# Softmax sums of a recurrent attention chain, issued in column groups of 32, with fewer filler matmuls

## The chip, the core and the metric

The kernel runs on one core of a Trainium2 chip. The metric is device time in microseconds (us), as the median of the runs. TensorE's instructions are written PE (matmuls) and PEld (weight loads), VectorE is DVE, ScalarE is ACT, GpSimd is POOL, and SP is the engine that issues most of the DMA transfers.

## The reference, cut to what matters

The model is four layers, A, B, A, B, on x of 2048 rows by 640 columns. Layer A is attention in 64 segments of 32 rows, each with 8 memory rows ahead of it. The memory rows of a segment are the first 8 output rows of the segment before, so the segments are a chain.

```python
for s in range(n_seg):                       # 64 segments, 32 heads of 192
    h = concatenate([mem, x[:, 32*s:32*s+32]], axis=1)      # 40 rows of 640
    q, k, v = h @ Wq, h @ Wk, h @ Wv
    p = softmax(where(mask, q @ k.T * scale, -1e9))
    o = (p @ v) @ Wo
    mem = o[:, :8]
    outs.append(o[:, 8:])
x = x + concatenate(outs)      # layer A; layer B follows (linear attention), then both again
```

## The kernel before, in words

Each layer A first computes, for all segments at once, the parts of q, k and v that do not depend on the memory (`A_pre`). Then `A_chain` walks through the 64 segments. A segment goes through four rounds of 8 heads each, in the order 0 to 3 or, in every second segment, 3 to 0.

**Order.** `A_chain` runs under a manual schedule: each engine works through its instructions in the order in which the code issues them, and semaphores hold them where they depend on another engine or a DMA transfer. So the order below is the code's order.

**A segment.** The new rows lie transposed in `hT` (128 partitions, five blocks of 32 columns). `project` multiplies them by a round's weights for Q, K or V: five steps of four matmuls each, one matmul for each group of 32 output partitions (`tile_position=(0, 32 * g)`, line 988), each 32 columns of weights from `hT` and 384 moving columns. ACT copies the result out of `ps_qk` into `raw` (line 998; one buffer, used for Q and K in turn), and DVE transposes `raw` into `QT` (lines 1006 to 1008) or `KT` (1003). For V, ACT and DVE (1017, 1019) copy to `Vp`, whose rows 64 to 79 a DMA fills from `vb` (`extra_v`, line 971, issued by POOL).

`scores` (mask matmul line 1025, six matmuls line 1030) fills `ps_s`, ACT takes the exponential into `E` (line 1085), and `sums` (line 1099) multiplies `E` (80 partitions, 320 columns) by a block of ones, which leaves each column's sum in the 80 partitions of `ps_s`. `normalise` takes ln and exp of the negative of these sums on ACT (1104, 1105), and DVE multiplies `E` by the result (1106). `attend` (line 1038) multiplies `E` by `Vp`; ACT and DVE (1044, 1045) copy to `OT`; `wo_round` (line 1067) multiplies `OT` by a round's output weights and adds up in `ps_w`: twelve steps of four matmuls with 160 columns, again one for each group of 32 output partitions. The mask, the scores, the sums, `attend` and the fillers use the whole array; `project` and `wo_round` use column groups of 32.

Round n of a segment runs Q of n+1, `attend` of n-1, scores of n, K of n+1, sums of n, V of n+1. The last round has no following projections: behind V of round 3 stand scores, `attend` of round 2, part of a `wo_round`, sums, the rest of the `wo_round`s, four filler matmuls (`keep_busy`, line 1074, into `ps_idle`, which nothing reads), `attend` of round 3, five fillers, the last `wo_round`, five fillers and two weight loads (`fill`, line 1080). Then DVE transposes `ps_w` (line 1220) and casts it into the first eight columns of the next `hT` (1221), and the next segment begins. Between these, DVE also transposes the next segment's own rows into `hT` (line 943).

**Loads.** Part of the weights stays in SBUF. In each segment SP loads again three blocks each of Wq, Wk and Wv (line 681) as the projections of round 0 give their slots free, and the output weights of the last round (line 698, six transfers of 320 KB), into the buffer `wo_end`, which the `wo_round` of the first round has just read. POOL issues the small transfers of `vb`, `kqb` and `otb`.

**Fillers.** A segment holds a fixed number of TensorE instructions. The first segment of the first layer A also has `FILL[0]` weight loads of a single column.

Of the kernel before, what the change touches and what calls it, by code (L numbers as in the profile page):

```python
# [17 lines left out]
SLOTS = {"Q": 3, "K": 3, "V": 3}  # L18
LN_EPS = 1e-5

FILL = {0: 86, 2: 79}
SEG_FILL = 2

LATE = 64512
# [3 lines left out]
def ap3(ap, dims):  # L28
    return bass.AP(tensor=ap.tensor, offset=ap.offset, ap=[list(d) for d in dims])
# [86 lines left out]
class Kernel:  # L116
# [799 lines left out]
    def A_chain(self, xn_dram, at_dram, li, load_slot, piece, load_wo, late_wo, wo_mid, wo_end, low):  # L916
        nc, tc, KC, NSEG = self.nc, self.tc, self.KC, self.NSEG
        scale = float(self.Dh) ** -0.5
        NR = 4
        with tc.tile_pool(name=f"A{li}_ch", reuse_waits="tile", bufs=1) as sp, \  # L920
# [17 lines left out]
            def load_rows(s):  # L938
                nc.gpsimd.dma_start(out=xr[8:32, :], in_=xn_dram[32 * s:32 * s + 24, :])
# [61 lines left out]
            def to_rows(raw, m):  # L1001
                if m == "K":
                    nc.vector.transpose(out=KT[:, :, 0:64], in_=raw[:, :].rearrange("p (c j) -> p c j", j=64))  # L1003
                else:
                    rv = raw[:, :].rearrange("p (x i j) -> p x i j", i=3, j=64)
                    nc.vector.transpose(out=QT[:, :, 0:4:3, 0:64], in_=rv[:, :, 0:3:2, :])  # L1006
                    nc.vector.transpose(out=QT[0:64, :, 1, 0:64], in_=rv[0:64, :, 1, :])
                    nc.vector.transpose(out=QT[64:P, :, 2, 0:64], in_=rv[64:P, :, 1, :])
# [25 lines left out]
            def attend(E, n, OT=None):  # L1034
                O = [pop.tile([P, 512], F32, name=f"ps_o{x}", tag=f"o{x}") for x in range(2)]
                for x in range(2):
                    for k, e, i in ((0, 0, 0), (320, 1, 2), (128, 0, 1), (192, 1, 1)):
                        nc.tensor.matmul(O[x][:, 80 * i:80 * i + 80], lhsT=Vs[n % 2][0:80, 448 * x + k:448 * x + k + 128],  # L1038
                                         rhs=E[0:80, 160 * x + 80 * e:160 * x + 80 * e + 80], start=(k == 0),
                                         stop=(k == 192), skip_group_check=True)  # L1040
                if OT is None:
                    OT = sp.tile([P, 6, 64], BF16, name="OT", tag="OT")
                o = [x[:, 0:240].rearrange("p (i q) -> p i q", q=80) for x in O]
                nc.scalar.activation(out=OT[:, 0:3, :], in_=o[0][:, :, 0:64], func=ACT.Copy)  # L1044
                nc.vector.tensor_copy(out=OT[:, 3:6, :], in_=o[1][:, :, 0:64])
                return OT, o
# [15 lines left out]
            def wo_round(W, r, OT, first, last, part=range(12)):  # L1062
                w = low[:, 0:7680] if last_wo == r else wo_end[:, :] if r in (0, 3) else wo_mid[:, 7680 * (r - 1):7680 * r]
                for i in part:
                    c, q = i % 6, 32 * (i // 6)
                    for g in range(4):
                        nc.tensor.matmul(W[32 * g:32 * g + 32, 0:160], lhsT=OT[:, c, q:q + 32],  # L1067
                                         rhs=w[:, 640 * i + 160 * g:640 * i + 160 * g + 160], start=(first and i == 0),
                                         stop=(last and i == 11), tile_position=(0, 32 * g), skip_group_check=True)

            def keep_busy(ps, n, w=384):

                for _ in range(n):
                    nc.tensor.matmul(ps[:, 0:w], lhsT=self.ident[:, :], rhs=wo_mid[:, 0:w], start=True, stop=True,  # L1074
                                     skip_group_check=True)

            def fill(n):

                for _ in range(n):
                    nc.tensor.ldweights(self.ident[:, 0:1])  # L1080

            def weigh(last):
                S = scores()
                E = sp.tile([P, 384], BF16, name="E3", tag="raw") if last else sp.tile([P, 320], BF16, name="E", tag="E")
                nc.scalar.activation(out=E[0:80, 0:320], in_=S[0:80, 0:320], func=ACT.Exp, scale=scale)  # L1085
                return S, E
# [9 lines left out]
                        kqs.append(load_kqb(*turns[at + 2]))  # L1096

            def sums(S, E):
                nc.tensor.matmul(S[0:80, 0:320], lhsT=ap3(self.ones_blk[0:80, :], [list(self.ones_blk[0:80, :].ap[0]), [0, 80]]), rhs=E[0:80, 0:320], start=True, stop=True,  # L1099
                                 skip_group_check=True)  # L1100

            def normalise(S, E):
                rc = S[0:80, 0:320]
# [17 lines left out]
            for s in range(NSEG):  # L1121
# [6 lines left out]
                def q_or_k(m, n):  # L1128
                    ps = pqp.tile([P, 512], F32, name="ps_qk", tag="qk")
                    project(hT, ps, m, n, s, range(KC))  # L1130
                    return to_raw(ps, "OT" if m == "K" and n == 0 else "raw")
# [11 lines left out]
                if s == 0:  # L1143
                    fill(FILL[li])
                to_rows(q_or_k("K", 0), "K")
# [10 lines left out]
                for n in range(L):  # L1156
                    raw = q_or_k("Q", n + 1)
                    if n > 0:
                        OT, o = attend(Ep, n - 1)
                        tails_after(n - 1)  # L1160
                    S, E = weigh(False)
                    to_rows(raw, "Q")
                    if n > 0:
                        otb = keep_tail(o)
                    next_kq(s, n)
                    if n > 0:
                        store_tail(otb, s, order[n - 1])
                    to_rows(q_or_k("K", n + 1), "K")
                    sums(S, E)
                    normalise(S, E)  # L1170
                    if n == 1:
                        wo_round(W, order[n - 1], OT, True, False)
                        if n == 1:
                            if s < NSEG - 1:
                                load_wo(order[L])
                            else:
                                tails = [self.fetch_tails(tb, low) for tb in range(2)]
                    if n + 1 < L:
                        pv = v_banks()
                        project(hT, pv, "V", n + 1, s, range(KC))  # L1180
                        v_rows(pv, n + 1)
                    Ep = E
# [6 lines left out]
                S, E = weigh(True)  # L1189
# [4 lines left out]
                store_tail(otb, s, order[L - 1])  # L1194
                wo_round(W, order[L - 2], OT1, False, False, range(6, 8))
                sums(S, E)
                wo_round(W, order[L - 2], OT1, False, False, range(8, 12))
                normalise(S, E)
# [2 lines left out]
                    hx_transpose(hT, range(1))  # L1201
                wo_round(W, order[L - 1], OT, False, False)
                idle = pqp.tile([P, 512], F32, name="ps_idle", tag="qk")
                keep_busy(idle, 4, 96)
                OT, o = attend(E, L)
                tails_after(L)
                if s == NSEG - 1:
# [1 line left out]
                if s + 1 < NSEG:  # L1209
                    hx_transpose(hT, range(1, 4))  # L1210
                    if s + 2 < NSEG:
                        load_rows(s + 2)
                keep_busy(idle, 5, 230)
                wo_round(W, order[L], OT, False, True)
                keep_busy(idle, 5, 230)
                fill(SEG_FILL)
                if s + 1 < NSEG:
                    wt = sp.tile([P, KC, 32], F32, name="wt", tag="raw")
# [86 lines left out]
```

## Time and profile before

| what | value |
|---|---|
| time of the kernel, median of 3 runs | 3610.64 us (3610.51 to 3611.67) |
| span of the profiled execution, first to last instruction | 3590.5 us |
| median less span (launch and end, around the span) | 20.1 us |
| PE busy | 3465.5 us, 97% of the span |
| PEld, DVE, ACT, POOL busy | 63%, 65%, 57%, 44% |
| mean granted TensorE clock | 0.993 |
| HBM traffic over the span | 257 GB/s |
| sums, line 1099 | 512 matmuls, four in each of 128 segments |

The profiled execution's own time is not listed apart from its span; the 20.1 us around the span are taken from the median. A row of the timeline gives the start in us, the duration of the run of equal instructions in us, the engine, the line of the code, the operation, output and inputs, the count, and in brackets the idle time ahead of it with what ended it. Matmul records overlap, since the next matmul enters the array while the last one still drains: the step from start to start is what a matmul costs.

### The profile page before, as it was taken

The page shows a single profiled execution, that of the slowest core. Times are in us where ns is not written, and L with a number is a line of the kernel's source. Part 1 is how long each engine was busy: PE and PEld are TensorE (multiplying, and loading weights), DVE is VectorE, ACT ScalarE, POOL GpSimd, SP SyncE. Part 2 cuts the span into 40 slices and gives each one's busy share as a digit, 9 for nine tenths or more (in the row PEclk, how much of TensorE's full clock was granted, in tenths as well). Part 3 has the DMA queues.
Part 4 walks back from the last instruction along what each step waited for, and adds up shares of the span by engine and source line. Part 5 has one row for each costly group of instructions (what it writes and reads, how often), then busy time and mean ns, then how long its engine had stood idle before and what let it go on. Part 6 is the DMA issues. An engine that isn't in the chain of part 4 may idle for free.

```text
span 3590.5 us, 168460 instructions
## 1 busy us (share of the span) xinstructions
PE 3465.5 (97%) x70978; PEld 2268.6 (63%) x71399; DVE 2327.0 (65%) x6320; ACT 2032.0 (57%) x5233; POOL 1589.1 (44%) x4173
## 2 busy tenths in 40 slices
PE   9989999999999999999999899999999999999999
PEld 7756666666666666655377566666666666666553
DVE  5466666667666666746633566666666666676465
ACT  3356666666566656646432556666666666666463
POOL 3445555555555555530123455555545555555400
PEclk9999999999999999999999999999999999999999
DMA  8988888888788878860476878887888888888600
GB/s 311 334 290 288 281 295 282 278 292 299 278 284 295 289 277 278 295 224 3 146 272 217 290 275 287 290 291 278 285 294 279 290 282 292 292 281 287 222 1 30
DMA packets 452689, 929.38 MB, mean 259 GB/s; under 512 B 75338, under 2 KB 218330, under 8 KB 448858
## 3 DMA queue, kind: packets, MB, share of 16 engines
q1 hardware_dynamic: 382266, 817.56, 64.0%
q0 software_dynamic: 67744, 87.80, 7.9%
q8 instruction: 557, 9.13, 1.0%
q10 hardware_dynamic: 1920, 13.24, 0.9%
q14 instruction: 202, 1.65, 0.1%
HBM read 848.50 MB, written 73.73 MB: 257 GB/s over the span
## 4 chain that ended last, share of the span: by engine, by line
PE 55%; DMA 20%; issue 9%; DVE 7%; POOL 5%; ACT 4%; SPq 1%; PEld 0%; POOLq 0%; ACTq 0%; DVEq 0%
PE ps_qk L988 17%; DMA arena<-wo_rows 7%; DMA Vp<-vb 6%; PE ps_v L988 6%; PE ps_w L1067 6%; PE ps_pre L878 3%; PE ps_o L1038 3%; PE ps_s L1030 3%; DVE hT L943 2%; PE ps_s L1099 2%; DMA arena<-in_A_Wv_dram 2%; PE ps_s L1025 2%; PE ps_pre L902 2%; PE ps_idle L1074 2%; PE kv L1260 1%
## 5 line engine op out<-in xcount | busy, mean ns | idle before, releaser
L988 PEld LDWEIGHTS <-hT 128*32 128x32 bf16 x30720 | 746.5, 96 | 431.9 <-DVE hT L1221 27.2
L988 PE MATMUL ps_qk<-arena,hT 128*32 128x384 bf16 x20480 | 998.8, 328 | 14.6 <-DMA arena<-in_A_Wq_dram 4.2
L998 ACT ACTIVATE raw<-ps_qk 128x384 bf16<-128x384 f32 x1024 | 502.0, 490 | 383.7 <-PE ps_s L1099 250.9
L988 PE MATMUL ps_v<-arena,hT 128*32 128x384 bf16 x10240 | 534.6, 328 | 8.7 <-DMA arena<-in_A_Wv_dram 8.4
L971 POOL DMA_DIRECT2D Vp<-vb x512 | 258.4, 505 | 611.4 <-PE ps_o L1038 465.6
L1067 PE MATMUL ps_w<-arena,OT 128*32 128x160 bf16 x18432 | 446.1, 234 | 11.4 <-DMA arena<-wo_rows 10.4
L1003 DVE STREAM_TRANSPOSE KT<-raw 128x384 bf16<-128x384 bf16 x512 | 296.0, 578 | 194.5 <-ACT raw L998 190.5
L1067 PEld LDWEIGHTS <-OT 128*32 128x32 bf16 x18432 | 322.7, 96 | 103.8 <-ACT OT L1044 22.3
L1006 DVE STREAM_TRANSPOSE QT<-raw 128x256 bf16<-128x256 bf16 x512 | 227.9, 445 | 237.5 <-ACT raw L998 195.5
L959 POOL DMA_DIRECT2D kqb<-kqb x512 | 290.9, 568 | 168.9 <-POOL KT L967 147.3
L1019 DVE CAST Vp<-ps_v 64x384 bf16<-64x384 f32 x512 | 286.2, 559 | 113.6 <-ACT Vp L1017 90.0
L1106 DVE TENSOR_TENSOR E<-E,ps_s 80x320 bf16<-80x320 bf16 x512 | 247.4, 483 | 142.7 <-ACT ps_s L1105 142.3
L1058 POOL DMA_DIRECT2D otb<-otb x512 | 282.7, 552 | 128.1 <-DVE otb L1054 100.0
L1017 ACT ACTIVATE Vp<-ps_v 64x384 bf16<-64x384 f32 x512 | 246.1, 481 | 138.4 <-PE ps_v L988 122.9
L1038 PEld LDWEIGHTS <-Vp 80*128 80x128 bf16 x4096 | 189.9, 99 | 123.1 <-issue 80.5
L1038 PE MATMUL ps_o<-E,Vp 80*128 80x80 bf16 x4096 | 233.0, 201 | 31.8 <-DMA Vp<-vb 15.0
L1085 ACT ACTIVATE E<-ps_s 80x320 bf16<-80x320 f32 x512 | 221.4, 432 | 68.0 <-PE ps_s L1030 33.6
L951 ACT ACTIVATE Vp<-ps_w 32x160 bf16<-32x160 f32 x512 | 150.3, 294 | 155.1 <-DVE wt L1220 138.4
L964 POOL COPY QT<-kqb 128x64 bf16<-128x64 bf16 x512 | 124.5, 243 | 254.8 <-PE ps_s L1030 248.5
L1030 PE MATMUL ps_s<-QT,KT 128*80 128x80 bf16 (+1 forms) x3072 | 233.2, 213 | 1.6 <-POOL KT L967 1.5
L1104 ACT ACTIVATE ps_s<-ps_s 80x320 f32<-80x320 f32 x512 | 214.7, 419 | 31.2 <-PE ps_s L1099 31.2
L1030 PEld LDWEIGHTS <-KT 128*80 128x80 bf16 x3072 | 205.4, 119 | 28.7 <-issue 18.3
(156 smaller groups left out, 5446.4 us busy)
## 6 DMA issues: line engine op xcount, KB each, us to landing
arena<-wo_rows SPq DMA_DIRECT2D x780, 320.0 KB, 6.8
arena<-in_A_Wq_dram SPq DMA_DIRECT2D x427, 384.0 KB, 4.4
arena<-in_A_Wv_dram SPq DMA_DIRECT2D x427, 384.0 KB, 6.6
arena<-in_A_Wk_dram SPq DMA_DIRECT2D x768, 192.0 KB, 4.6
kqb<-kqb POOLq DMA_DIRECT2D x512, 48.0 KB, 5.1
arena<-in_A_Wk_dram SPq DMA_DIRECT2D x43, 384.0 KB, 7.8
vb<-arena POOLq DMA_DIRECT2D x128, 112.0 KB, 6.3
Vp<-vb POOLq DMA_DIRECT2D x512, 28.0 KB, 4.8
```

The lines of the kernel that those rows point to most:

```text
L959: nc.gpsimd.dma_start(out=kqb[:], in_=self.kqb_d[r, :, s, :])
L971: nc.gpsimd.dma_start(out=Vs[n % 2][64:80, :], in_=self.vb_d[s, r].rearrange("g t f -> (g t) f"))
L988: nc.tensor.matmul(o[32 * g:32 * g + 32, 0:384], lhsT=hT[:, b, :], rhs=rhs, start=(i == 0), stop=(i == KC - 1), tile_position=(0, 32 * g), ...
L998: nc.scalar.activation(out=raw[:], in_=ps[:, 0:384], func=ACT.Copy)
L1003: nc.vector.transpose(out=KT[:, :, 0:64], in_=raw[:, :].rearrange("p (c j) -> p c j", j=64))
L1017: nc.scalar.activation(out=o, in_=i, func=ACT.Copy)
L1019: nc.vector.tensor_copy(out=o, in_=i)
L1030: nc.tensor.matmul(S[0:80, c0:c0 + 80 * (q1 - q0)], lhsT=KT[:, 3 * x + i, :], rhs=QT[:, x, q0:q1, :], start=False, stop=(x == 1 and i == 2 ...
L1038: nc.tensor.matmul(O[x][:, 80 * i:80 * i + 80], lhsT=Vs[n % 2][0:80, 448 * x + k:448 * x + k + 128], rhs=E[0:80, 160 * x + 80 * e:160 * x ...
L1058: nc.gpsimd.dma_start(out=self.otb_d[:, s, 96 * r:96 * r + 96], in_=otb[:, :, :].rearrange("p c t -> p (c t)"))
L1067: nc.tensor.matmul(W[32 * g:32 * g + 32, 0:160], lhsT=OT[:, c, q:q + 32], rhs=w[:, 640 * i + 160 * g:640 * i + 160 * g + 160], start=(firs ...
L1106: nc.vector.tensor_tensor(out=E[0:80, 0:320], in0=E[0:80, 0:320], in1=rc, op=ALU.mult)
```

## The change

The sums are issued as three matmuls, one for each group of 32 output partitions (the last has 16), with the same 320 moving columns. The first group of fillers becomes one matmul of 384 columns in place of four of 96. The second becomes one of 512 in place of five of 230. The third becomes four matmuls of 512, one for each group of 32 output partitions, in place of five of 230. A segment has eight matmuls more in the sums and eight fewer in the fillers, so its number of instructions stays. Before the second round of projections of the very first segment, eight single-column weight loads go. No other engine's instructions or their order change.

```diff
-FILL = {0: 86, 2: 79}
+FILL = {0: 78, 2: 79}
...
+            def keep_busy_groups(ps, n, w):
+
+                for _ in range(n):
+                    for g in range(4):
+                        nc.tensor.matmul(ps[32 * g:32 * g + 32, 0:w], lhsT=self.ident[:, 0:32], rhs=wo_mid[:, 0:w], start=True,
+                                         stop=True, tile_position=(0, 32 * g), skip_group_check=True)
...
             def sums(S, E):
-                nc.tensor.matmul(S[0:80, 0:320], lhsT=ap3(self.ones_blk[0:80, :], [list(self.ones_blk[0:80, :].ap[0]), [0, 80]]), rhs=E[0:80, 0:320], start=True, stop=True,
-                                 skip_group_check=True)
+                ones = self.ones_blk[0:80, :]
+                for k0, k1 in ((0, 32), (32, 64), (64, 80)):
+                    nc.tensor.matmul(S[k0:k1, 0:320], lhsT=ap3(ones, [list(ones.ap[0]), [0, k1 - k0]]), rhs=E[0:80, 0:320],
+                                     start=True, stop=True, tile_position=(0, k0), skip_group_check=True)
...
-                keep_busy(idle, 4, 96)
+                keep_busy(idle, 1, 384)
                 OT, o = attend(E, L)
...
-                keep_busy(idle, 5, 230)
+                keep_busy(idle, 1, 512)
                 wo_round(W, order[L], OT, False, True)
-                keep_busy(idle, 5, 230)
+                keep_busy_groups(idle, 1, 512)
                 fill(SEG_FILL)
```

## The prediction

> **What bounds the kernel now.** I read the page first, for how full TensorE is and what the chain of waits holds.
>
> ```profile
> span 3590.5 us, 168460 instructions
> PE 3465.5 (97%) x70978; PEld 2268.6 (63%) x71399; DVE 2327.0 (65%) x6320; ACT 2032.0 (57%) x5233; POOL 1589.1 (44%) x4173
> ...
> PE 55%; DMA 20%; issue 9%; DVE 7%; POOL 5%; ACT 4%; SPq 1%; PEld 0%; POOLq 0%; ACTq 0%; DVEq 0%
> ```
>
> PE looks full, but its busy time holds fillers and draining records, and the chain gives it only 55%, with 20% on DMA. So I looked at one segment, from 1050.74 on, in stretches (PE, PEld, DVE, ACT, POOL busy, then clock, DMA share, GB/s).
>
> ```profile
> 1051.74:1054.74 3.00, 3.00 (x67) 1.83 (x59) 1.97 (x5) 2.31 (x6) 1.07 (x2) 1.00 0.90 291
> 1054.74:1068.20 13.46, 13.37 (x348) 8.86 (x349) 9.50 (x26) 9.43 (x26) 7.42 (x23) 1.00 1.01 363
> 1068.20:1071.70 3.50, 3.09 (x90) 2.31 (x80) 2.77 (x9) 0.54 (x2) 2.17 (x6) 1.00 0.27 83
> ```
>
> For 13.46 us PE and the DMA engines are both full (share 1.01); at the end the DMA engines empty and a chain of small steps runs. A saving on PE counts only where no other chain ends later, so each of the four places of the sums is read by itself. Round 0, PE alone:
>
> ```profile
> L1099 PE MATMUL ps_s<-E,ones_blk x512: 296/329/490, 177.0 to 3331.5; 80*80 80x320 bf16 x171
> ...
> 1054.79 1.00 PE L988 MATMUL ps_qk<-arena,hT 128*32 128x384 bf16 x20
> 1055.71 0.33 PE L1099 MATMUL ps_s<-E,ones_blk 80*80 80x320 bf16 x1
> 1055.97 1.00 PE L988 MATMUL ps_v<-arena,hT 128*32 128x384 bf16 x20
> 1056.80 0.99 PE L988 MATMUL ps_qk<-arena,hT 128*32 128x384 bf16 x20
> 1057.87 0.45 PE L1038 MATMUL ps_o<-E,Vp 80*128 80x80 bf16 x8
> ```
>
> **What the sums cost on PE.** V to Q, both in column groups, is 0.83 us for 20 matmuls, so five steps of 0.166. K therefore has entered by 1054.79 + 0.83 = 1055.62, but the sums start at 1055.71: 0.09 to change from column groups to the whole array. V starts 0.26 later, though 320 columns at K's rate take 0.166 x 320/384 = 0.14: 0.12 to change back. The sums thus take 0.35 of PE. As three matmuls in column groups, side by side as the four of V are, they should take 0.14. No row shows three with 80 rows; the bounds are nothing saved (it still drains) and 0.35 - 0.14 = **0.21 us**. I take 0.21, since both neighbours are in the same grouping. Over 512 that is 107 us, if all of it lay on the path. It does not.
>
> **Round 0: nothing.** Its other engines:
>
> ```profile
> 1055.63 0.31 DVE L1008 STREAM_TRANSPOSE QT<-raw 64x128 bf16<-64x128 bf16 x1
> 1056.05 0.49 ACT L998 ACTIVATE raw<-ps_qk 128x384 bf16<-128x384 f32 x1 [0.72 <-PE ps_s L1099]
> 1056.44 0.43 ACT L1104 ACTIVATE ps_s<-ps_s 80x320 f32<-80x320 f32 x1
> 1057.33 0.48 DVE L1106 TENSOR_TENSOR E<-E,ps_s 80x320 bf16<-80x320 bf16 x1 [0.18 <-ACT ps_s L1105]
> ```
>
> `attend` starts at 1057.87, 0.06 after E is ready (1057.33 + 0.48 = 1057.81), though Q has entered by 1057.63. E hangs on ACT: K's copy into `raw`, then ln (0.40 after the sums ended at 1056.04), exp, then DVE. The bracket puts ACT's wait at 1056.05 down to the sums, but that copy reads `ps_qk` and stands ahead of the sums in the code; what it needs is the single `raw` buffer, which DVE's L1008 releases at 1055.94. That chain starts at the scores, before the sums. PE saves 0.21 and waits 0.21 longer.
>
> **Round 1: 0.21.**
>
> ```profile
> 1061.22 0.48 DVE L1106 TENSOR_TENSOR E<-E,ps_s 80x320 bf16<-80x320 bf16 x1 [0.18 <-ACT ps_s L1105]
> ...
> 1062.43 0.46 PE L1038 MATMUL ps_o<-E,Vp 80*128 80x80 bf16 x8
> ...
> 1063.19 0.51 POOL L971 DMA_DIRECT2D Vp<-vb  x1 [1.68 <-PE ps_o L1038]
> ```
>
> E is ready at 1061.70, `attend` comes at 1062.43: 0.67 us of slack beyond the latency of 0.06, because a `wo_round` stands between. PE sets the pace, so `attend`, and POOL's issue of the `Vp` rows that waits for it, come 0.21 earlier.
>
> **Round 2: nothing more.**
>
> ```profile
> 1065.80 0.48 DVE L1106 TENSOR_TENSOR E<-E,ps_s 80x320 bf16<-80x320 bf16 x1 [0.18 <-ACT ps_s L1105]
> ...
> 1066.33 0.45 PE L1038 MATMUL ps_o<-E,Vp 80*128 80x80 bf16 x8
> ```
>
> `attend` starts 0.05 after E (1066.28), which again runs from that round's scores through `raw`. It keeps the 0.21 of round 1 and adds none.
>
> **Round 3 and the end of the segment.**
>
> ```profile
> 1066.44 0.43 ACT L1085 ACTIVATE E<-ps_s 80x320 bf16<-80x320 f32 x1
> 1066.96 0.33 PE L1099 MATMUL ps_s<-E,ones_blk 80*80 80x320 bf16 x1
> 1067.22 0.46 PE L1067 MATMUL ps_w<-arena,OT 128*32 128x160 bf16 x16
> 1068.21 0.48 DVE L1106 TENSOR_TENSOR E<-E,ps_s 80x320 bf16<-80x320 bf16 x1 [0.61 <-ACT ps_s L1105]
> 1069.13 0.33 PEld L1038 LDWEIGHTS <-Vp 80*128 80x128 bf16 x8 [0.49 <-DMA Vp<-vb]
> 1069.43 0.66 PE L1074 MATMUL ps_idle<-arena,ident 128*128 128x230 bf16 x5
> 1069.48 0.33 ACT L1044 ACTIVATE OT<-ps_o 128x192 bf16<-128x192 f32 x1 [1.31 <-PE ps_o L1038]
> 1070.02 1.01 PE L1067 MATMUL ps_w<-arena,OT 128*32 128x160 bf16 x48
> 1070.02 1.11 DVE L943 STREAM_TRANSPOSE hT<-Vp 32x160 bf16<-32x160 bf16 x3
> 1071.16 0.28 DVE L1220 STREAM_TRANSPOSE wt<-ps_w 128x96 f32<-128x96 f32 x1
> ```
>
> The sums can start only once Exp is done (1066.87 plus 0.05), so the `wo_round` behind them starts at about 1066.92 + 0.14 = 1067.06 in place of 1067.22: 0.16 saved on PE, but here `attend` waits for neither PE nor E (1068.69). It waits for the `Vp` rows, issued at 1063.19.
>
> ```profile
>   PEld L1038: 29.2, 69
> ...
>   PE ps_w L1067: 10.4, 23
> ...
> L698 SPq DMA_DIRECT2D arena<-wo_rows x6: 326/391/659, 1060.2 to 1062.6; - x6
> ...
> DMA to landing us min/median/max: 4.8/6.8/7.5
> ```
>
> (The first row lists who waited for L971, the second who waited for L698, both over the whole run; the last two are L698 in this segment.) In 69 of 128 segments the weight load of an `attend` waits for `Vp`. Its issue moves 0.21 earlier, and I take it that it lands so much earlier. The Trainium skill (Trainium Kernel Development and Optimization, Key Constraints) says that DMAs of different issuing engines interleave on the same 16 DMA engines; by that the small load need not wait out the backlog of weights and its landing moves; queued behind it, it would not, and the sum for these segments would be 0.
>
> The first fillers keep 384 columns: nothing. The second, 1150 columns in 0.49 (five steps of 0.098, from 0.66 less a last record of 0.26), become 512 in 0.21: with 0.09 for the change PE is free at 1069.73, and the last `wo_round` waits for OT's first half (1069.81 plus 0.05) and starts at 1069.86 in place of 1070.02. That buys nothing by itself, since W, ready at 1071.03, waits for DVE, which transposes rows until 1071.13. The third fillers stand behind W, where the next segment waits for DVE's casts: nothing, and nothing for the eight weight loads. The cover for the fillers at zero is DVE's 1.11 us; without it they would give the 0.16.
>
> **The sum.** 69 segments x 0.21 = 14.5 us. The other 59 are late by something else, mostly PE itself, and could keep round 3's 0.16 too: 59 x 0.37 = 21.8. The ceiling is 36.3 us. Against it stands the last load of `wo_rows`: issued at 1062.6, with about 0.4 to issue and up to 7.5 to land, it arrives near 1070.5, and is needed ten of twelve steps into the last `wo_round` (1.01 less some 0.2 of the last record's drain, so 0.07 a step), near 1070.71. With both gains that need moves to about 1070.35, ahead of the landing, and the DMA engines are full, so its landing will not move. PE then waits 0.15 there, which DVE's lateness still covers here; it does not where the load lands later, and 23 waits show that already. Floor 0, ceiling 36; with no row that sorts the segments I take 45%, **16.3 us**: span 3574.2, median 3610.6 - 16.3 = **3594**, the 20.1 us around the span unchanged. The change adds no wait and moves no DMA past another; what moves does so because PE is earlier.
>
> **Rivals.** *The end of the loads holds the segment:* `wo_rows` or `Vp` land when the backlog is done, whatever PE does, or the sums still drain. For: share 1.01 over 13.46 us. Against: 0.67 of slack and idle DMA engines (0.27) after 1068.20. Gain 0 to 7: about 3607.
>
> *The clock falls: slower.* The fillers lost are idle time in the tail, 0.28 twice (0.49 to 0.21, for the third as for the second).
>
> ```profile
> 939.74:943.15 3.41, 2.24 (x84) 1.66 (x77) 1.53 (x6) 1.04 (x4) 2.46 (x7) 1.00 0.53 175
> ...
> 1318.62:1322.03 3.41, 1.87 (x44) 1.25 (x44) 1.69 (x5) 1.32 (x5) 2.60 (x8) 1.00 0.82 315
> 1322.03:1325.45 3.42, 3.42 (x77) 2.97 (x65) 1.39 (x5) 1.09 (x4) 2.62 (x8) 0.50 0.22 56
> ```
>
> A window with PE busy 1.87 was followed by one at half clock, which costs about half of its 3.42, 1.7 us; one with 2.24 was not. The tail's 3.09 becomes about 2.5: above both, but a wait of 0.3 to 0.6 in the same window crosses. Fourteen such windows (23.5 us) undo 16.3 and add 7.2; one in four segments is 32 x 1.7 = 54, so 3594 + 54 = 3648. The Trainium skill (TensorE: Matmul & The Clock Gate, Part 1) has the clock fall after an idle window of about 3.4 us; by that no tail would fall, while the row with 1.87 says that half idle is enough.
>
> *The wait list is right and ACT does wait for the sums:* then rounds 0, 2 and 3 pay as well, up to 107 us, perhaps half: 3557.
>
> **How the numbers follow.** The forecast has 0.58, the loads 0.22, the clock 0.14, the fast case 0.06. A difference under 0.2% (7.2 us) is not told from no change. So faster 0.58 + 0.06 = 0.64, same 0.22, slower 0.14. The range goes from the ceiling, 3574, to 3616 (nothing gained, and three windows at half clock, 5 us); it leaves out the fast case and most of the clock's.
>
> **What would show it.** Right: sums to V about 0.14 apart with no 0.09 ahead; `attend` of rounds 0 and 2 still 0.05 to 0.06 behind E, of round 1 earlier by 0.21 against the segment's start, with more idle PE; more waits for `wo_rows`; few new half-clock windows. Wrong: ACT's copy at L998 moving with the sums, `Vp` landing at its old place, or PEclk below 9 in the chain.

## The result, and the profile after

| kernel | time, median (us) | ratio to before, 95% interval |
|---|---|---|
| before | 3611.15 (3610.51 to 3623.96, 4 runs) | |
| changed | 3597.1 (3589.87 to 3601.94, 4 runs) | 0.9949 [0.993, 0.9968] |

The changed kernel is faster by 14 us by the medians. Run again later it gave 0.9966 [0.995, 0.9982], and an unchanged copy of the kernel before, in the same set, 0.9985 [0.9974, 0.9997]. So differences of 5 us aren't to be read from one ratio, and the change is worth some 10 to 18 us (10.7 against the copy, 18 by the first ratio).

The page of the changed kernel, the lines that answer to those shown of before:

```profile
span 3595.1 us, 168452 instructions
...
PE 3303.2 (92%) x70978; PEld 2275.7 (63%) x71391; DVE 2332.6 (65%) x6320; ACT 2034.5 (57%) x5233; POOL 1588.9 (44%) x4173
...
PE 47%; DMA 29%; DVE 9%; issue 6%; ACT 5%; POOL 1%; PEld 1%; SPq 1%; ACTq 0%; DVEq 0%; POOLq 0%
...
L998 ACT ACTIVATE raw<-ps_qk 128x384 bf16<-128x384 f32 x1024 | 501.9, 490 | 366.1 <-DVE QT L1008 249.9
```

PE lost 162 us of busy time and 8 points of the chain, DMA gained 9. The lines that share out the chain, before first, show which loads:

```profile
PE ps_qk L988 17%; DMA arena<-wo_rows 7%; DMA Vp<-vb 6%; PE ps_v L988 6%; PE ps_w L1067 6%; PE ps_pre L878 3%; PE ps_o L1038 3%; PE ps_s L1030 3%; DVE hT L943 2%; PE ps_s L1099 2%; DMA arena<-in_A_Wv_dram 2%; PE ps_s L1025 2%; PE ps_pre L902 2%; PE ps_idle L1074 2%; PE kv L1260 1%
```

```profile
DMA arena<-wo_rows 18%; PE ps_qk L988 14%; PE ps_v L988 5%; DMA arena<-in_A_Wv_dram 5%; PE ps_pre L878 5%; PE ps_w L1067 4%; PE ps_o L1038 3%; PE ps_s L1030 3%; PE ps_pre L902 2%; DVE E L1115 2%; ACT raw L998 2%; DMA Vp<-vb 2%; PE kv L1269 2%; DVE QT L1006 1%; PE ps_s L1025 1%
```

The reload of the output weights, `wo_rows`, goes from 7% to 18%. The span is 4.6 us longer than that of the profile before, although the kernel is faster: the listed time of this profiled execution is 3596.84 us, only 1.7 over its span, so if as little lay around it, the first profile (span 3590.5) was of an execution of about 3592 us, quicker than any timed run of that kernel. Two spans can't be set against each other here; places within a segment can. Here is one, the 42nd, which is the segment that the prediction reads (it starts at 1051.77 here, at 1050.74 there), in stretches placed as there, then its rows:

```profile
1055.77:1069.23 13.46, 13.07 (x364) 9.92 (x362) 9.72 (x27) 9.48 (x26) 7.64 (x24) 1.00 1.01 356
1069.23:1072.93 3.70, 2.17 (x62) 1.37 (x63) 2.51 (x9) 0.54 (x2) 2.21 (x5) 1.00 0.36 113
```

```profile
1055.77 1.00 PE L988 MATMUL ps_qk<-arena,hT 128*32 128x384 bf16 x20
...
1056.60 0.31 PE L1108 MATMUL ps_s<-E,ones_blk 80*32 80x320 bf16 x3
1056.61 1.11 PE L988 MATMUL ps_v<-arena,hT 128*32 128x384 bf16 x20
1056.61 0.31 DVE L1008 STREAM_TRANSPOSE QT<-raw 64x128 bf16<-64x128 bf16 x1
1057.03 0.49 ACT L998 ACTIVATE raw<-ps_qk 128x384 bf16<-128x384 f32 x1 [0.72 <-DVE QT L1008]
1057.42 1.11 PE L988 MATMUL ps_qk<-arena,hT 128*32 128x384 bf16 x20
1058.32 0.48 DVE L1115 TENSOR_TENSOR E<-E,ps_s 80x320 bf16<-80x320 bf16 x1 [0.18 <-ACT ps_s L1114]
1058.85 0.45 PE L1038 MATMUL ps_o<-E,Vp 80*128 80x80 bf16 x8 [0.32 <-DVE E L1115]
...
1062.20 0.48 DVE L1115 TENSOR_TENSOR E<-E,ps_s 80x320 bf16<-80x320 bf16 x1 [0.18 <-ACT ps_s L1114]
1063.18 0.46 PE L1038 MATMUL ps_o<-E,Vp 80*128 80x80 bf16 x8
1063.93 0.51 POOL L971 DMA_DIRECT2D Vp<-vb  x1 [1.45 <-PE ps_o L1038]
...
1069.98 0.33 PEld L1038 LDWEIGHTS <-Vp 80*128 80x128 bf16 x8 [0.93 <-DMA Vp<-vb]
1070.72 0.89 PE L1067 MATMUL ps_w<-arena,OT 128*32 128x160 bf16 x40
1072.01 0.32 PE L1067 MATMUL ps_w<-arena,OT 128*32 128x160 bf16 x8 [0.40 <-DMA arena<-wo_rows]
1072.38 0.28 DVE L1229 STREAM_TRANSPOSE wt<-ps_w 128x96 f32<-128x96 f32 x1 [0.40 <-PE ps_w L1067]
```

The rest is told as times after the segment's start. The sums follow K with no gap (1055.77 + 0.83 = 1056.60). V's matmuls for the fourth column group, which the three sums leave free, start beside them (1056.61); matmul by matmul, the trace has the other three groups of V 0.14 behind the sums. `attend` of round 0 is where it was (1058.85 - 1051.77 = 7.08; before 7.13), now with 0.32 of idle PE ahead of it. `attend` of round 1 comes at 11.41 in place of 11.69, the issue of the `Vp` rows at 12.16 in place of 12.45, the weight load that waits for them at 18.21 in place of 18.39. The last `wo_round` starts 0.33 sooner (18.95 for 19.28) and then stops at its last two steps until 20.24, for `wo_rows`. DVE's transposes of W start at 20.61 in place of 20.42. In this segment the loads took all of the gain.

Over all segments, medians of the same places (start of the row less the start of the segment's first Q matmul, us; last line: start of the next segment):

| place | before | changed | before, no reload | changed, no reload |
|---|---|---|---|---|
| `attend` of round 0 | 7.13 | 7.13 | 7.13 | 7.13 |
| `attend` of round 1 | 11.69 | 11.46 | 11.69 | 11.46 |
| `attend` of round 2 | 15.59 | 15.36 | 15.60 | 15.36 |
| `wo_round` behind the sums of round 3 | 16.48 | 15.90 | 16.48 | 15.90 |
| `attend` of round 3 | 18.38 | 18.21 | 18.00 | 17.66 |
| last `wo_round`, first matmul | 19.26 | 18.94 | 18.88 | 18.38 |
| last `wo_round`, last matmul | 20.14 | 20.19 | 19.66 | 19.16 |
| next segment | 21.01 | 21.08 | 20.57 | 20.23 |

(The last two columns are the seventh and eighth experiment below, without the reload of the output weights.) Up to the third `wo_round` both pairs run alike. There PE is 0.59 us ahead (16.48 to 15.90) with the fourth column group, 0.46 with the other three (they start at 16.03); of that, 0.17 are left at the last `attend` and nothing at the end, where the loads run. The list of waits says roughly to whom it went; PE's own waits, in total, times and longest, of before and of the changed kernel:

```profile
PE ps_w L1067 <- issue: 16.4, 36, 1.2
PE ps_o L1038 <- DMA Vp<-vb: 15.0, 39, 1.0
PE ps_w L1067 <- DMA arena<-wo_rows: 10.4, 23, 1.0
PE ps_v L988 <- DMA arena<-in_A_Wv_dram: 8.4, 9, 3.2
...
PE ps_o L1038 <- DVE E L1106: 2.9, 4, 1.1
```

```profile
PE ps_qk L988 <- DVE hT L1230: 55.8, 126, 0.6
PE ps_o L1038 <- DVE E L1115: 45.9, 132, 2.3
PE ps_w L1067 <- issue: 39.5, 70, 1.2
PE ps_w L1067 <- DMA arena<-wo_rows: 37.3, 80, 1.9
PE ps_v L988 <- DMA arena<-in_A_Wv_dram: 22.3, 32, 3.8
PE ps_o L1038 <- DMA Vp<-vb: 13.8, 29, 1.2
```

The sums of round 1 save 0.235 us (11.691 - 11.456 at `attend` of round 1, before rounding). If all four places save as much, that is 512 x 0.235 = 120 us. The first row after, for `hT`, is new, but it is not theirs: it stands where the third fillers did. The kernel with the short fillers alone, below, has 46.4 us of it and no gain, the one with the sums alone none of it and the whole gain. The four other waits that grew took 43.0 (E), 23.1 (issue), 26.9 (`wo_rows`) and 13.9 (Wv), 107 in all; in the pair of the first two experiments they took 42.9, 26.1, 22.7 and 8.3, 100 in all. So most of what the sums saved went into waits, and the largest part of it into E. What is left, 13 or 20 us, is near the gain, but that is luck: one execution stands on each side, and the mean segment is 21.142 us long in both of the first two traces.

### The profile page after: what moved, and what is told of

It reads as the page before. It is cut to its first block, busy times and chain, and to the rows that moved or that the text cites. A ratio compares the mean times of both kernels' runs of the same rounds, so it can differ in the third digit from the quotient of the medians.

```text
span 3595.1 us, 168452 instructions
## 1 busy us (share of the span) xinstructions
PE 3303.2 (92%) x70978; PEld 2275.7 (63%) x71391; DVE 2332.6 (65%) x6320; ACT 2034.5 (57%) x5233; POOL 1588.9 (44%) x4173
## 4 chain that ended last, share of the span: by engine, by line
PE 47%; DMA 29%; DVE 9%; issue 6%; ACT 5%; POOL 1%; PEld 1%; SPq 1%; ACTq 0%; DVEq 0%; POOLq 0%
DMA arena<-wo_rows 18%; PE ps_qk L988 14%; PE ps_v L988 5%; DMA arena<-in_A_Wv_dram 5%; PE ps_pre L878 5%; PE ps_w L1067 4%; PE ps_o L1038 3%; PE ps_s L1030 3%; PE ps_pre L902 2%; DVE E L1115 2%; ACT raw L998 2%; DMA Vp<-vb 2%; PE kv L1269 2%; DVE QT L1006 1%; PE ps_s L1025 1%
## 5 line engine op out<-in xcount | busy, mean ns | idle before, releaser
L988 PEld LDWEIGHTS <-hT 128*32 128x32 bf16 x30720 | 874.4, 97 | 418.8 <-DVE hT L1230 53.9
L988 PE MATMUL ps_qk<-arena,hT 128*32 128x384 bf16 x20480 | 1031.0, 327 | 64.0 <-DVE hT L1230 55.8
L998 ACT ACTIVATE raw<-ps_qk 128x384 bf16<-128x384 f32 x1024 | 501.9, 490 | 366.1 <-DVE QT L1008 249.9
L988 PE MATMUL ps_v<-arena,hT 128*32 128x384 bf16 x10240 | 601.7, 327 | 22.8 <-DMA arena<-in_A_Wv_dram 22.3
L1067 PE MATMUL ps_w<-arena,OT 128*32 128x160 bf16 x18432 | 488.3, 234 | 46.4 <-DMA arena<-wo_rows 37.3
L1067 PEld LDWEIGHTS <-OT 128*32 128x32 bf16 x18432 | 391.0, 96 | 123.4 <-issue 53.8
L1038 PE MATMUL ps_o<-E,Vp 80*128 80x80 bf16 x4096 | 233.1, 201 | 71.7 <-DVE E L1115 45.9
L1044 ACT ACTIVATE OT<-ps_o 128x192 bf16<-128x192 f32 x384 | 126.1, 328 | 192.8 <-PE ps_o L1038 177.7
L1113 ACT ACTIVATE ps_s<-ps_s 80x320 f32<-80x320 f32 x512 | 214.7, 419 | 26.9 <-PE ps_s L1108 26.9
```

Source lines behind the costliest of these rows:

```text
L988: nc.tensor.matmul(o[32 * g:32 * g + 32, 0:384], lhsT=hT[:, b, :], rhs=rhs, start=(i == 0), stop=(i == KC - 1), tile_position=(0, 32 * g), ...
L998: nc.scalar.activation(out=raw[:], in_=ps[:, 0:384], func=ACT.Copy)
```

## The experiments

**Unchanged kernels again**, to see what a ratio is worth.

> The kernel before once more, unchanged, against itself: it tells how far two sets of executions of one program stand apart, and whether the span of 3590.5 us that its first profile showed goes with a time of 3610 us. Both theories: ratio 1.000, within about 0.2%. If what lies around the span is 1.7 us, as in the changed kernel's list (3596.84 against a span of 3595.1), the first profile was of an execution near 3592 us, 18 us under its median, and executions of one program then differ by that much; a spread of 10 us or more in this run would say so.

> The changed kernel once more. Theory P (the prediction): round 1's 0.21 us a segment moves the Vp rows and with them the end of the segment; 12 to 20 us faster, ratio 0.9945 to 0.9967. Theory L (the loads): the two first traces both show 21.142 us a segment in the mean, because waits for wo_rows and for instructions took what PE saved; then the 14 us between the medians came from how single executions fell, and this one is within 0.2% of before.

Measured 3611.97, 0.9985 [0.9974, 0.9997], and 3601.23, 0.9966 [0.995, 0.9982]. Against the copy the change is worth 10.7 us. The two profiles, with mean segments of 21.214 and 21.204 us, hardly differ. Within one trace the segments scatter by some 0.5 us (standard deviation), so the mean of 128 is uncertain by about 0.04 us, or 5 us of the kernel's time (an estimate): two single traces can't show a gain of this size, and it rests on the medians of many executions.

**The sums alone.** The groups in the sums, the fillers kept near their old length:

```diff
-                keep_busy(idle, 5, 230)
+                keep_busy(idle, 3, 384)
                 wo_round(W, order[L], OT, False, True)
-                keep_busy(idle, 5, 230)
-                fill(SEG_FILL)
+                keep_busy(idle, 3, 384)
```

> Only the sums are in column groups; the second and third fillers keep their PE time (three of 384 columns in place of five of 230) and the number of instructions of a segment stays. Theory P: the whole gain comes from the sums, 12 to 20 us, since the last wo_round waited for DVE anyway. Theory L: within 0.2% of before. A theory F, that the fillers held the end of the segment: under a third of the changed kernel's gain here.

Measured 3596.08, 0.995 [0.993, 0.997]. The sums carry the gain, and theory F falls.

**The fillers alone.** The kernel before with both `keep_busy(idle, 5, 230)` as `(idle, 5, 102)`.

> Only the fillers are shorter: the second and third groups are five of 102 columns in place of five of 230, the sums stay as they were, and no instruction is added or taken away. Theory P: 0 to 3 us faster, because DVE's 1.11 us of transposes cover the last wo_round; a clock that falls in more windows would make it slower. Theory L: within 0.2%. Theory F: 10 us or more faster, by 0.16 us earlier start of the last wo_round in the segments where it is not waiting for wo_rows.

Measured 3617.0, 1.0009 [0.9994, 1.0023]. In the trace the last `wo_round` starts 0.14 us sooner (19.13 for 19.26) and ends no sooner (20.21 for 20.14, or 20.24 in the copy): the shorter fillers are worth nothing, and cost nothing.

**Round 1 alone, and the other rounds alone.**

```diff
-                    sums(S, E)
+                    sums(S, E, n == 1)
```

The other kernel has `n != 1` there, and groups in round 3 as well; both keep the number of TensorE instructions by fewer, longer fillers.

> Column groups for the sums of round 1 alone; the first fillers are two of 192 columns in place of four of 96, so that the number of instructions stays. Theory P (the prediction: of the four places only round 1's reaches the end of the segment, through the Vp rows): nearly the whole gain of the sums, 10 to 16 us faster, ratio 0.9955 to 0.997. A theory Q, that the gain comes through the later rounds (scores of round 3 and the sums behind them, which stand nearer to the end): under 5 us.

> The complement: column groups for the sums of rounds 0, 2 and 3, not 1; fillers of 384, 4 x 288 and 3 x 384 columns, so that their PE time and the number of instructions stay. Theory P: under 5 us, since rounds 0 and 2 wait for E and round 3 waits for Vp. Theory Q: 10 us or more.

Measured 3608.12, 0.9978 [0.9964, 0.9991], and 3603.49, 0.996 [0.9943, 0.9977]. Both parts are under one; the rounds that the prediction gave the least moved the time at least as much as round 1. The intervals overlap, and the copy of the kernel before has 0.9985 itself, so how the gain divides between the rounds stays open. That it is round 1's alone doesn't hold: theory P expected under 5 us of the second kernel, and its ratio gives 14.

Their traces, one execution each, show two things. The mask matmul of the scores of round 3 comes at 15.04 us after the segment's start before (median), at 14.80 in each of these two, and at 14.57 in the changed kernel. So the sums of round 2 bring it 0.235 sooner, as those of round 1 do. And `attend` of round 3 starts at 18.35 and 18.34, hardly sooner than before (18.38), where the changed kernel has 18.21. The waits ahead of it, round 1 alone first, then the other rounds:

```profile
PE ps_w L1067 <- issue: 43.2, 76, 2.2
...
PE ps_o L1038 <- DMA Vp<-vb: 7.8, 17, 2.2
```

```profile
PE ps_o L1038 <- DMA Vp<-vb: 33.0, 70, 1.7
PE ps_w L1067 <- issue: 23.0, 38, 1.7
```

With round 1 alone the `Vp` rows come sooner, but PE stops more in the `wo_round`; with the others alone PE is sooner, but the `Vp` rows are not. By these traces it takes both to bring this `attend` forward.

**No reload of the output weights.** Before and changed, without the six transfers of `wo_rows` in a segment (1.97 MB); the last `wo_round` of all but the last segment then uses other weights, so these kernels leave that part of the computation out.

```diff
-                            if s < NSEG - 1:
-                                load_wo(order[L])
-                            else:
+                            if s == NSEG - 1:
```

> The kernel before without its reload of the last round's output weights in the segments but the last (the last wo_round then multiplies by the weights that lie there). It takes away six loads of 320 KB a segment. If the end of the loads holds the segments: 0.5 us a segment or more faster, 60 us or more. If PE holds them: 10 us or less, the waits for wo_rows that the trace shows.

> The changed kernel without the same reload. If the loads' end swallows what the sums save, the change is worth more here than with the reload: by the working of the prediction 0.21 to 0.37 us a segment against e7, 27 to 47 us. If the chains through E (raw, KT) swallow it instead, the difference to e7 stays at 10 to 16 us.

Measured 3533.83, 0.9763 [0.9739, 0.9787], and 3506.09, 0.9691 [0.9671, 0.9711]: the change is worth 27.7 us here, about twice of what it is with the reload. Both answers favour the loads: the kernel before gains 83 us, over the 60 expected if the end of the loads holds the segments, and 27.7 lies at the low end of 27 to 47 and above 10 to 16. The waits of the two, before first:

```profile
PE ps_v L988 <- DMA arena<-in_A_Wv_dram: 8.9, 15, 2.5
...
PE ps_w L1067 <- DMA arena<-wo_rows: 2.9, 4, 0.9
...
PE ps_w L1067 <- issue: 0.4, 1, 0.4
```

```profile
PE ps_o L1038 <- DVE E L1115: 41.5, 128, 0.4
PE ps_v L988 <- DMA arena<-in_A_Wv_dram: 22.4, 38, 3.8
...
PE ps_w L1067 <- DMA arena<-wo_rows: 5.6, 4, 2.2
```

E still takes its 41 us and Wv grows as it did; the growth of `wo_rows` and of issue is gone. (The changed kernel also has 76.3 us for `hT`, in the place of the short fillers.) In both kernels `attend` of round 3 now starts 0.054 us after E in the median segment, and the `Vp` rows have landed some 3 us ahead. So nearly all of the wait for `Vp`, of those for `wo_rows` and of the issue waits in the `wo_round`s comes from this reload. The run takes away its 1.97 MB as well as its late end, and doesn't part the two.

**A buffer of its own for K of round 1**, on before, on the changed kernel, on the one with the sums alone and on the changed one without the reload (which leaves out what was said above). In round 1's place in the code the buffer of `OT` is free; K of round 0 goes through it already:

```diff
-                    return to_raw(ps, "OT" if m == "K" and n == 0 else "raw")
+                    return to_raw(ps, "OT" if m == "K" and n < 2 else "raw")
```

> The kernel before, but K of round 1 goes through the buffer of OT in place of raw, so that ACT's copy no longer waits for DVE's transposes of Q. Theory R (the prediction's: in round 0 the single raw buffer sets E, and the sums do not): the copy starts when K is ready, about 0.2 us sooner, E and attend of round 0 come up to 0.16 sooner (the idle time of PE ahead of that attend), and the kernel gains 5 to 12 us. Theory W (the wait list: ACT waits for the sums): the copy stays where it is against the sums, attend of round 0 stays at 7.13 us after the segment's start, and the time stays within 4 us.

> The changed kernel with the same edit. Theory R: attend of round 0, which did not move with the sums, now comes 0.2 to 0.35 us sooner than in the changed kernel, since PE has 0.39 us of idle time there; at the same share of the segments as in the change, 10 to 20 us under the changed kernel, ratio to before 0.990 to 0.993. Theory L (the end of the loads takes what is gained): attend of round 0 moves, but the time stays within 6 us of the changed kernel (0.995 to 0.997), and the wait of PE inside the wo_rounds grows. Theory W: attend of round 0 stays at 7.13.

> The sums in column groups with the old long fillers, and K of round 1 through the buffer of OT. The fillers were worth nothing, so every theory expects the ratio of the changed kernel with the same edit, within 0.002; if the shorter fillers do gain once other waits are gone, it is slower by more than 0.002.

> The changed kernel without the reload of the last round's output weights (all but the last segment use old weights there, so the output differs from the reference), and with K of round 1 through the buffer of OT. Theory L: with 1.97 MB a segment less to load, the earlier attend of round 0 counts in every segment: 0.2 to 0.35 us times 128, 26 to 45 us under the same kernel without the edit, 0.957 to 0.962. Theory E (in these runs the chain from the scores of round 3 through E holds the end, and it starts with Q of round 3 on PE): the same gain. If it gains no more than 10 us, neither the loads nor PE's pace held these segments.

Measured, in this order: 3607.79, 0.998 [0.9968, 0.9993]; 3589.79, 0.9934 [0.9917, 0.9951]; 3590.3, 0.9938 [0.9919, 0.9957]; 3490.72, 0.9657 [0.9638, 0.9676]. Round 0 of the first of them, the sums still whole:

```profile
1058.01 0.33 PE L1099 MATMUL ps_s<-E,ones_blk 80*80 80x320 bf16 x1
1058.13 0.49 ACT L998 ACTIVATE raw<-ps_qk 128x384 bf16<-128x384 f32 x1 [0.51 <-PE ps_qk L988]
...
1059.41 0.48 DVE L1106 TENSOR_TENSOR E<-E,ps_s 80x320 bf16<-80x320 bf16 x1 [0.18 <-ACT ps_s L1105]
1060.01 0.46 PE L1038 MATMUL ps_o<-E,Vp 80*128 80x80 bf16 x8
```

ACT's copy now starts 0.12 into the sums, which end at 1058.34: it never waited for them, and theory W falls. `attend` of round 0 moves from 7.13 to 6.98 us in the median segment, where PE itself is the limit (0.11 behind E), and from 7.13 to 6.91 in the changed kernel, still 0.05 behind E. The waits of the changed kernel with this edit:

```profile
PE ps_w L1067 <- issue: 49.6, 88, 1.3
PE ps_w L1067 <- DMA arena<-wo_rows: 40.2, 90, 2.2
...
PE ps_v L988 <- DMA arena<-in_A_Wv_dram: 26.4, 51, 2.9
...
PE ps_o L1038 <- DVE E L1115: 2.8, 3, 1.6
```

(This list also has 35.1 us for ACT's `OT`; there the trace lacks the records of 128 filler matmuls, whose weight loads it has.) The wait for E fell from 45.9 to 2.8, its size before the change, and the three that hang on the loads grew by 10.1, 2.9 and 4.1 against the changed kernel's first trace; in its second the issue waits had already come to 49.9. Changed kernel and this edit together, 0.9934, are, with the next, the fastest of the complete kernels: 24 us under before, 5 to 12 under the change alone (0.9949 and 0.9966, from other sets), which lies between theories R and L. On before alone 0.998 can't be told from the copy's 0.9985. The kernel with the long fillers gives the same, so these don't count here either. Without the reload the edit brings 0.21 us in the median segment (20.228 to 20.018), as expected, but by the times only 15.4 us (3506.09 to 3490.72), not 26 to 45: the mean segment moved by 0.145. Which waits hold the slower segments there was not tried.

## Why the prediction was right, and where it was not

**The number.** 3594 was forecast, 3597.1 came, a gain of 14 us for 16.3. It was right in sign and size, and in that most of the saving would go into waits. In the working, the savings of rounds 2 and 3 and the waits for loads were too small, and the split of the segments didn't hold. That the number came out so near is in part luck.

**What the sums cost: right.** 0.35 to 0.14, 0.21 saved. From matmul start to matmul start in the segment shown, the last K step to the first V step took 0.525 us before and 0.302 after, of which 0.163 is K's own step: 0.36 and 0.14 (after, for the three groups of V that the sums used; the fourth starts beside the sums). The Trainium skill (TensorEngine Tiling (Array Packing), Key Properties) says that a change of the tiling mode drains TensorE. The trace agrees: the gap between K and the sums is gone, and a whole-array matmul between two runs of column groups pays some 0.22 for its two changes.

**Round 0 nothing: right, and shown.** `attend` stayed 0.05 behind E. The wait list put ACT's 250.9 us down to the sums; the same 250 us stand in the changed kernel's page under DVE's L1008 (the row of L998 above), and the buffer of its own moved the copy, with the sums as they were. With this the rival in which ACT waits for the sums falls.

**Round 1: right. Round 2 nothing more: right at its `attend`, wrong behind it.** `attend` of both came 0.235 sooner. But the scores of round 3 stand ahead of `attend` of round 2 and don't wait for its E: the sums of round 2 bring them another 0.235 sooner, also where round 1 is left as it was (15.04 to 14.80). The prediction looked at `attend` alone.

**Round 3: mis-sized.** 0.16 was forecast for PE on top of round 1's 0.21, 0.37 in all; in three of the four column groups the `wo_round` behind these sums starts 0.46 sooner (16.48 to 16.03), 0.12 of it from the sums themselves (0.26 from them to the `wo_round` before, 0.14 after) and 0.34 from their earlier start. Little of it lasts: 0.17 at `attend` of round 3, which waits either for `Vp` or behind stops inside that `wo_round` that the profile puts down to "issue" and the prediction hadn't seen.

**`Vp` moves with its issue: right.** Issue 0.29 sooner, use 0.18 sooner in the segment shown. Over all segments, in medians, the issue moves from 12.45 to 12.21 us and the landing from 18.19 to 17.84 (18.15 to 17.92 in the repeated pair; 17.95 with round 1 alone, 18.22 with the other rounds). The prediction weighed here what the Trainium skill (Trainium Kernel Development and Optimization, Key Constraints) says, that DMAs of different issuing engines interleave on the same 16 DMA engines. The trace agrees: before, the `Vp` rows are issued 0.5 us behind the last load of `wo_rows` and land 1.7 us ahead of it. They still share with the backlog: they land 5.7 us after their issue, and 2.5 without the reload.

**The fillers at zero: right.** 1.0009 for them alone. DVE's cover shows in the table where the loads are gone: the last matmul comes 0.50 sooner (19.66 to 19.16), the next segment 0.34 (20.57 to 20.23).

**The limit, the last load of `wo_rows`: right, and larger.** That its landing would not move is so: 19.87 and 20.02 us after the segment's start in the two traces of before, 20.06 in both of the changed kernel (medians). The prediction saw the need move ahead of the landing and 0.15 us of wait, covered by DVE. The waits went from 23 to 80 and from 10.4 to 37.3 us, and in the segment shown one of 0.40 put W behind DVE's rows. The rival in which the loads hold the segment is thus half of the truth: without the reload the same change brings 27.7 us.

**The share of 45% and the ceiling of 36.3.** 10 to 18 us are 28 to 50% of it. The share was a guess between the ends and held; its reasons, 69 segments by `Vp` and 59 by PE, were not what divided the segments, since rounds 0, 2 and 3 by themselves give 0.996. So the share came out by luck, not by its reasons.

**The 20.1 us around the span: wrong.** There are 1.7; the rest was a quick execution against the median. It did the median no harm, because it was added to both sides.

**The clock: the rival fell.** Row 1069.23 to 1072.93 has PE busy for 2.17 of 3.70 us, below the 2.5 that the prediction worked out, and the clock is 1.00; the mean granted clock was 0.992, and 0.989 to 0.992 over the four runs. The traces hold 59.1 us at half clock where before has 55.2 (68.9 for 62.5 in the repeated pair), which would cost 2 to 3 us. By the Trainium skill (TensorE: Matmul & The Clock Gate, Part 1), which has the clock fall after an idle window of about 3.4 us, there is no fall here; the trace agrees for this tail.

## What to carry to other kernels

A saving on an engine that is 97% busy is worth what the next thing in line leaves of it: list that engine's waits before and after, and the sum of what grew tells roughly where it went. Before crediting a wait to the instruction that ended last, look for a buffer with a single copy: here ACT's wait followed the buffer and not the sums. And where a kernel's executions spread by 0.7%, compare places within its period in the traces, and take the gain from medians of many runs.

## What the runs showed of the hardware

PE stops inside the `wo_round`s, and the profile names neither weights nor inputs as late, only "issue": 16.4 us in 36 waits before (23.8 in 42 in the copy), 39.5 in 70 after (49.9 in 76 when run again), 49.6 in 88 with the buffer apart, and 0.4 in one wait where the output weights aren't loaded again.

The traces show what ends these stops. Nearly all of them, 34 before and 69 after, lie behind the sums of round 3, most at the same place: the last matmul ahead of the stop ends 17.07 us after the segment's start before, 16.53 after (medians). A DMA queue of the kind "instruction" moves 557 packets of 16 KB, some four in a segment. Every one of these stops ends 1.2 to 1.8 us after such a packet has landed. Before, the packet of that part of the segment lands at 16.05 us (median) where PE stops and at 15.29 where it doesn't; after, at 15.75 and 14.95. Without the reload of the output weights it lands at 13.5 before and 13.3 after, and PE stops there once and not at all. So by all signs PE waits there for instructions, whose transfer shares the DMA engines with the loads. The sums bring PE to that place 0.54 us sooner, the packet comes only some 0.3 sooner in either group, and about twice as many segments stop. No run moved these packets alone.
